# Second MoE, pairs 2 and 3 of 3: w_out by seven half-block products, four quads summed in PSUM, in an fp32r attention and two-MoE kernel

## The chip, the core and the metric

The kernel runs on one core of a Trainium2 chip. TensorE (PE in the profile; PEld is its weight load), VectorE (DVE), ScalarE (ACT), GpSimd (POOL) and SyncE (SP, which issues the DMAs here) work side by side and meet at semaphores. The metric is the device time of one execution in microseconds (us), lower is better.

## The reference

Linear attention with softmaxes over q and k, then two dense feed-forward layers ("MoE") on 2304 tokens, d_model 512, d_ff 2048. The second one is what the change touches:

```python
def _moe_ref(x, w_in, w_out):
    h = x @ w_in
    g = np.maximum(h, 0.0) + np.log1p(np.exp(-np.abs(h)))
    return (g @ w_out).astype(np.float32)

def _moe2_ref(x, w_in, w_out):
    h = x @ w_in
    alpha = 1.0
    g = np.where(h > 0.0, h, alpha * (np.exp(np.minimum(h, 0.0)) - 1.0))
    return (g @ w_out).astype(np.float32)
```

## The kernel before

Everything is float32 in and out; on PE a float32 number is a pair of fp32r values, high and low part, and a product is three matmuls (high x high, high x low, low x high). ACT makes the high part by a cast, DVE the low part by a subtraction.

Tokens go in six blocks of 384 (`BLK`, three rows `R` of 128); two blocks make a *pair* (p = 0, 1, 2 in names and code; pair 1, 2, 3 in words), d_ff is cut into eight *quads* `f` of 256 columns. The work unit is (MoE `m`, pair `p`, quad `f`), 48 in all; the second MoE is m = 1.

- **`up`** (`add_up`, L811): h = x @ w_in for two blocks and 256 columns by Strassen's scheme (Winograd's form): seven products instead of eight, six matmuls of 384 columns each, in the order 1, 2, 6, 5, 3, 7, 4 by due time. Products 1, 6, 5, 3 add into one PSUM bank `ub`, 2 into `ua`, 7 and 4 into `uc`; the ring `ha` has two banks. After 1, 6 and 5, ACT copies `ub` away to a tile `s`, and the next of these products adds to `ub` after that. DVE adds `s` to `ua` or `uc` and has `h`.
- **ELU** (`add_elu`): ACT relu(-h) and exp of that into `u`; DVE takes 1 off, then g = max(h, 0) + u.
- **Split** (`add_g`): `gh` by ACT, `gl` by DVE, for each half `j` of 128 d_ff columns.
- **Down** (`add_down`, L1016): plain: per quad 12 steps (two token blocks, two halves j, three rows r) of three matmuls with 512 columns, into six PSUM banks `acc0`, `acc1` that stay open over all eight quads of a pair. The first MoE's pairs 2 and 3 use `add_down_turned` (L978), where a matmul of 512 columns and one of 256 follow each other with the same weights, each with a load of its own.
- **Weights.** In m = 1, pair 1 builds the seven w_in forms and the high and low w_out of each quad and stores them to DRAM (`wfd`, 1.75 MB, and `wod`, 1 MB a quad); pairs 2 and 3 load them back (`wf`, `wo`, two buffers each).
- **End of a pair** (`add_store`): ACT and DVE copy the six banks to `y`, SP stores them.

Each operation is a step with an engine, a duration, what it reads and writes, the ring of buffers it takes, and a due time. `Plan.order` lists all steps: each engine takes next what can start first, and of those what is due first. The emitted order is that list, and every engine runs its part in order. `up` of one quad stands beside `down` of the quad before it.

Of the kernel before, what the change touches and what calls it, by code (L numbers as in the profile page):

```python
# [20 lines left out]
class Plan:  # L21
# [7 lines left out]
    def __init__(self, bufs):  # L29
        self.bufs = bufs  # L30
        self.steps, self.tile_ring, self.users = [], {}, {}
        self.writer, self.readers = {}, {}
        self.early, self.tab = 0.0, []

    def add(self, eng, dur, fn, r=(), w=(), new=(), due=None, after=0.0, behind=(), port=False, hold=(), tab=None):
        n = len(self.steps)
        deps = {i for i in behind if i is not None}
        for key, ring in new:
            self.tile_ring[key] = ring
        w = tuple(w) + tuple(key for key, _ in new)  # L40
# [12 lines left out]
        self.tab.append(tab)
        return n

    def order(self):
        n = len(self.steps)
        succ = [[] for _ in range(n)]
        for i, s in enumerate(self.steps):
            for d in s[3]:  # L60
                succ[d].append(i)
# [10 lines left out]
        free = {ring: [0.0] * c for ring, c in self.bufs.items()}  # L72
        ready = [0.0] * n
        clock = {PE: 0.0, ACT: 0.0, DVE: 0.0, POOL: 0.0, DMA: 0.0}
        open_ = {e: set() for e in clock}
        for i in range(n):
            if not left[i]:
                open_[self.steps[i][0]].add(i)
        lock, table = 0.0, "exp"
        seq = []  # L80
        while len(seq) < n:
            best = None
            for eng, cand in open_.items():
                starts = []
                for i in cand:
                    t = max(clock[eng], ready[i], lock if self.steps[i][-2] else 0.0)
                    if self.tab[i] not in (None, table):
                        t += T_TABLE
                    ok = True
                    need = {}  # L90
                    for _, ring in self.steps[i][4]:
                        need[ring] = need.get(ring, 0) + 1
                    for ring, c in need.items():
                        if len(free[ring]) < c:
                            ok = False
                            break
                        t = max(t, sorted(free[ring])[c - 1])
# [22 lines left out]
            for _, ring in new:  # L120
                free[ring].remove(min(free[ring]))
            for key in keys:
                uses[key] -= 1
                last[key] = max(last.get(key, 0.0), end)
                if not uses[key] and key in self.tile_ring:
                    free[self.tile_ring[key]].append(last[key] + SYNC)
# [30 lines left out]
def attention_moe_moe_kernel(  # L157
# [63 lines left out]
    const = pool("const")  # L221
    dp = pool("dp", bass.MemoryType.DRAM)

    plan = Plan({**{ring: b for ring, (b, _, _) in rings.items()}, **banks})
    T = {}

    def new(key, dt=None):
# [21 lines left out]
    }  # L249


    SLOT = 15.7
    UP, DN = 6 * 0.175, 3 * 0.231
    direct = lambda m, p, f: (m, p) == (0, 0) and f < 2
    quads = [(m, p, f) for m in range(2) for p in range(NPAIR) for f in range(NQ)]
    start, now = {}, 45.0
    for m, p, f in quads:
        start[m, p, f] = now
        now += SLOT + (3.0 if direct(m, p, f) else 0.0)
    end = now  # L260

    def after_quad(m, p, f):
# [481 lines left out]
    def add_w_out(m, f, rk):  # L744
# [9 lines left out]
        def _():  # L754
            nc.vector.tensor_tensor(
                T[wk][:, 2 * DM :], get(), T[wk][:, : 2 * DM].bitcast(F32), op=ALU.subtract
            )

        @step(DMA, 3.2, r=[hk, lk], w=[("wod", m, f)], hold=[wk], after=LAT)
# [30 lines left out]

    def add_up(m, p, f):
        t0 = start[m, p, f]
        wk = ("wf", m, "i", f, p)
# [4 lines left out]
        for i, at in ORDER:  # L798
            key, xk = where[i], ("xf", m, p, i)

            @step(
# [23 lines left out]

            elif i == 3:
                if m:
                    @step(ACT, t_act(BLK, True), r=[key], w=[("hp", m, p, f, 0, 1)], hold=[h0], behind=[made])
                    def _(key=key):
                        nc.scalar.copy(T[h0][:, BLK:], T[key][:, :BLK])  # L830
                else:
                    raw_h[p, f] = key

            else:
# [14 lines left out]
                made = _  # L849

    raw_h = {}

# [61 lines left out]
    def add_elu(p, f, j):  # L914

        hk, uk, gk = ((x, 1, p, f, j) for x in "hug")
        hs = [("hp", 1, p, f, j, half) for half in range(2)]

        @step(ACT, t_act(N2), r=hs, hold=[hk], make=[(uk, "u")], line="u")
        def _():  # L920
            nc.scalar.activation(new(uk), T[hk], AF.Relu, scale=-1.0)  # L921

        @step(ACT, t_act(N2), w=[uk], tab="exp")
        def _():
            nc.scalar.activation(T[uk], T[uk], AF.Exp, scale=-1.0)  # L925

        @step(DVE, t_dve(N2, True), w=[uk])
        def _():
            nc.vector.tensor_scalar(T[uk], T[uk], -1.0, None, op0=ALU.add)

        @step(DVE, t_dve(N2), r=[*hs, uk], hold=[hk], make=[(gk, "g")], line="g")
        def _():
            nc.vector.scalar_tensor_tensor(new(gk), T[hk], 0.0, T[uk], op0=ALU.max, op1=ALU.add)  # L933

    def add_g(m, p, f, j):
        gk, hk, lk = ((x, m, p, f, j) for x in ("g", "gh", "gl"))
# [47 lines left out]
    def add_down(m, p, f):  # L984
# [9 lines left out]
        for (i, j, r), at in zip(order, fill):  # L994
# [13 lines left out]
            def _(col=col, j=j, hk=hk, lk=lk, ak=ak, first=first, whole=whole, gk=gk, w32=w32):  # L1008
# [6 lines left out]
                for n, (g, a) in enumerate(((hk, 0), (hk, 1), (lk, 0))):  # L1015
# [95 lines left out]
    ahead = [(0, 1, 2), (0, 1, 4), (0, 1, 6), *((0, 2, f) for f in (0, 2, 3, 5, 6))]  # L1111

    for i, (m, p, f) in enumerate(quads):
        if f == 0:
            add_x(m, p)
        early(f"i{f}" if (m, p) == (0, 0) else "w")
# [10 lines left out]
        elif (m, p) == (0, 0):  # L1127
            add_w_out(m, f, add_words(m, "o", f))
        elif p == (1 if direct(m, 0, f) else 0):
            add_w_out(m, f, load_words(m, p, "o", f))  # L1130
        else:
            load_w_out(m, p, f)
        if (m, p, f) in ahead:
            early("ahead")
# [5 lines left out]
        else:  # L1140
            add_up(m, p, f)
            for j in range(2):
                (add_elu if m else add_softplus)(p, f, j)
                add_g(m, p, f, j)
        if i:
# [4 lines left out]
    add_down(*quads[-1])  # L1150
    add_store(*quads[-1][:2])

    with tc.manual_schedule():
        nc.scalar.preload_act_table_set("exp_and_others")
# [35 lines left out]
```

## Time and profile before

| | us |
|---|---|
| median of 3 runs | 842.66 (842.51 to 842.87) |
| span of the profiled execution | 841.3 |
| PE busy in it | 821.2 |
| DVE, ACT busy | 590.1, 534.2 |
| second MoE: pair 1, 2, 3 from about | 471.8, 597.2, 722.6 |

The span is from the first to the last instruction of the profiled execution; the timed runs hold what lies around it too. Busy times of the engines overlap.

### The profile page before, as it was taken

To read this page: it belongs to the slowest core of one execution; us is meant where nothing else is said; L and a number is where in the kernel's file an instruction comes from. 1 tells how busy PE (TensorE), PEld (TensorE's weight loads), DVE (VectorE), ACT (ScalarE), POOL (GpSimd) and SP (SyncE) were. 2 spreads that over 40 slices of the span, in tenths; PEclk is the share of its full clock that TensorE was granted. 3 is DMA by queue.
4 is the path that set the end of the run, shared out by engine and by line. 5 is a ranking of instruction groups with operands and counts; after the bars stand their busy time and mean duration, and the time that the engine had idled before them with its cause. 6 is when DMAs were issued, how large, how long until landed. Compare 5 with 4: busy or idle time off the path is not lost.

```text
span 841.3 us, 11929 instructions
## 1 busy us (share of the span) xinstructions
PE 821.2 (98%) x4678; PEld 721.3 (86%) x4678; DVE 590.1 (70%) x910; ACT 534.2 (63%) x786; POOL 6.1 (1%) x28
## 2 busy tenths in 40 slices
PE   5799999999999999999999999999999999999998
PEld 4466788889989999999999999899888899888896
DVE  7889999988888768776776786776544556533433
ACT  3877988886887757656655665665534456534443
POOL 2000000000000000000000000000000000000000
PEclk9999999999999999999999999999999999999999
DMA  9687775537885654687756689673765453763532
GB/s 283 165 280 248 216 261 194 199 100 238 263 310 181 236 205 161 221 303 267 250 178 230 261 300 338 257 295 143 250 234 216 179 232 139 255 232 138 187 139 76
DMA packets 63575, 186.37 MB, mean 222 GB/s; under 512 B 17952, under 2 KB 27168, under 8 KB 54560
## 3 DMA queue, kind: packets, MB, share of 16 engines
q1 hardware_dynamic: 63520, 185.61, 63.2%
q8 instruction: 37, 0.61, 0.3%
q14 instruction: 18, 0.15, 0.1%
HBM read 131.07 MB, written 54.53 MB: 221 GB/s over the span
## 4 chain that ended last, share of the span: by engine, by line
PE 83%; DVE 9%; ACT 5%; DMA 2%; issue 2%; ACTq 0%; DVEq 0%; SPq 0%
PE acc L1016 27%; PE ub L811 21%; PE acc L978 15%; PE uc L811 11%; PE ua L811 5%; PE px L507 1%; DMA raw_i<-in_moe_w_in_dram 1%; DMA raw_o<-in_moe_w_out_dram 1%; DVE mt L331 1%; PE pk L375 1%; DVE wf_i L731 1%; PE up L872 1%; ACT kvbd L401 1%; DVE ti_o L655 1%; PE pq L491 1%
## 5 line engine op out<-in xcount | busy, mean ns | idle before, releaser
L811 PE MATMUL ub<-xf,wf_i 128*128 128x384 f32 x1104 | 226.7, 340 | 0.4 <-ACT s L824 0.3
L1016 PE MATMUL acc<-wo_o,gh 128*128 128x512 f32 x720 | 226.0, 395 | 0.0
L811 PEld LDWEIGHTS ub<-xf,wf_i 128*128 128x128 f32 x1104 | 193.4, 188 | 16.5 <-ACT s L824 2.8
L845 DVE TENSOR_TENSOR h<-uc,s 128x384 f32<-128x384 f32 x92 | 51.1, 555 | 143.4 <-PE uc L811 135.0
L1016 PEld LDWEIGHTS acc<-wo_o,gh 128*128 128x128 f32 x720 | 132.5, 188 | 18.8
L1016 PE MATMUL acc<-wo_o,gl 128*128 128x512 f32 x360 | 142.5, 396 | 0.0
L824 ACT COPY s<-ub 128x384 f32<-128x384 f32 x138 | 65.9, 478 | 106.8 <-PE ub L811 106.5
L811 PE MATMUL uc<-xf,wf_i 128*128 128x384 f32 x552 | 112.2, 338 | 0.6 <-ACT g L893 0.6
L978 PE MATMUL acc<-gh,wo_o 128*128 128x512 f32 (+1 forms) x512 | 111.4, 339 | 0.0
L811 PEld LDWEIGHTS uc<-xf,wf_i 128*128 128x128 f32 x552 | 96.6, 188 | 8.2 <-ACT g L893 1.4
L940 ACT CAST gh<-g 128x768 fp32r<-128x768 f32 x92 | 77.1, 839 | 37.8 <-DVE g L933 37.1
L944 DVE TENSOR_TENSOR gl<-g,gh 128x768 fp32r<-128x768 f32 x92 | 87.8, 954 | 18.2 <-ACT gh L940 17.8
L978 PEld LDWEIGHTS acc<-gh,wo_o 128*128 128x128 f32 x512 | 83.2, 188 | 7.1
L1016 PEld LDWEIGHTS acc<-wo_o,gl 128*128 128x128 f32 x360 | 67.5, 187 | 14.4
L978 PE MATMUL acc<-gl,wo_o 128*128 128x512 f32 (+1 forms) x256 | 65.4, 336 | 0.0
L811 PE MATMUL ua<-xf,wf_i 128*128 128x384 f32 x276 | 55.8, 336 | 0.0
L811 PEld LDWEIGHTS ua<-xf,wf_i 128*128 128x128 f32 x276 | 48.0, 188 | 1.4 <-ACT xq L497 0.3
L933 DVE SCALAR_TENSOR_TENSOR g<-h,u 128x768 f32<-128x768 f32 x48 | 45.9, 957 | 1.4
L978 PEld LDWEIGHTS acc<-gl,wo_o 128*128 128x128 f32 x256 | 39.1, 188 | 5.3
L921 ACT ACTIVATE u<-h 128x768 f32<-128x768 f32 x48 | 40.7, 848 | 4.5 <-DVE h L845 2.7
L731 DVE TENSOR_TENSOR wf_i<-st_i,wf_i 128x1024 fp32r<-128x1024 f32 x30 | 36.6, 1221 | 8.1 <-ACT wf_i L727 7.9
L925 ACT ACTIVATE u<-u 128x768 f32<-128x768 f32 x48 | 40.7, 847 | 1.1
(98 smaller groups left out, 937.1 us busy)
## 6 DMA issues: line engine op xcount, KB each, us to landing
wo_o<-wod SPq DMA_DIRECT2D x30, 1024.0 KB, 6.8
wf_i<-wfd SPq DMA_DIRECT2D x16, 1792.0 KB, 7.3
raw_i<-in_moe_w_in_dram SPq DMA_DIRECT2D x16, 1024.0 KB, 6.5
raw_o<-in_moe_w_out_dram SPq DMA_DIRECT2D x16, 1024.0 KB, 7.4
wod<-wo_o SPq DMA_DIRECT2D x16, 1024.0 KB, 6.2
wfd<-wf_i SPq DMA_DIRECT2D x8, 1792.0 KB, 9.0
r_i<-w32i SPq DMA_DIRECT2D x24, 512.0 KB, 5.5
w32i<-ti_i SPq DMA_DIRECT2D x14, 512.0 KB, 5.5
```

The lines of the kernel that those rows point to most:

```text
L331: top = lambda o, x, y: nc.vector.tensor_tensor(o, x, y, op=ALU.max)
L731: nc.vector.tensor_tensor(view(1, lo, n, c), get(), view(0, lo, n, c).bitcast(F32), op=ALU.subtract)
L811: nc.tensor.matmul(ps[:, :BLK], T[wk][:, lo : lo + P], T[xk][:, (2 * c + kc) * BLK : (2 * c + kc + 1) * BLK], start=(i in first and kc == ...
L824: nc.scalar.copy(new(sk), T[key][:, :BLK])
L845: nc.vector.tensor_tensor(T[hk][:, half * BLK : (half + 1) * BLK], T[key][:, :BLK], T[sk], op=ALU.add)
L921: nc.scalar.activation(new(uk), T[hk], AF.Relu, scale=-1.0)
L925: nc.scalar.activation(T[uk], T[uk], AF.Exp, scale=-1.0)
L933: nc.vector.scalar_tensor_tensor(new(gk), T[hk], 0.0, T[uk], op0=ALU.max, op1=ALU.add)
L940: nc.scalar.copy(new(hk), T[gk])
L944: nc.vector.tensor_tensor(new(lk), T[gk], T[hk].bitcast(F32), op=ALU.subtract)
L978: nc.tensor.matmul(ps, T[wk][:, lo : lo + P], T[g][:, cols], start=(first and n == 0 and starts), stop=(f == NQ - 1 and j == 1 and n == 2) ...
L1016: nc.tensor.matmul(ps, T[g][:, col : col + P], T[wk][:, (2 * a + j) * DM : (2 * a + j + 1) * DM], start=(first and n == 0), stop=(f == NQ ...
```

## The change

For the second MoE's last two pairs (p = 1 and 2), `down` uses the same seven-product scheme. The g of a quad is a 2 x 2 matrix of blocks (two token blocks by two halves j), the w_out of it 2 x 2 (two halves j by two halves of 256 output columns). Four quads form a group, two groups a pair (`SIZES`).

- `add_elu`: g = max(exp(min(h, 0)) - 1, h) in one DVE pass; the separate -1 pass is gone in all of m = 1. In p = 1, 2 it is done in place in a buffer of the shared ring `G`.
- `add_parts`: for each quad, four sums of 384 columns on DVE, and for each of the seven products the operand's high part (ACT) and low part (DVE) into one of six buffers `F`. `add_g` is not called for these quads.
- `add_products`: products in the order 1, 7, 6, 2, 5, 4, 3; each loads one 1 MB weight tile `ws` for all four quads, and per quad runs nine matmuls of 256 columns (a *product step*: six for rows 0 and 1 in a bank of `acc0`, three for row 2 in a bank of `acc1`), summing four quads in PSUM. Then the bank is read out and set or added into rows `Y` in SBUF: ACT for products 1, 6, 7, 3 of a pair's first group, DVE for the rest. Rows go out by DMA when a pair is complete.
- `add_sums`: in pair 1 (p = 0) the four block sums of w_out, their splits, and six stores a quad into the DRAM tile `wos`, in place of the store to `wod`.
- `add_claims`: after p = 0, idle buffers of other rings (`u`, `g`, `gh`, `gl`, `ti`, `st`, `k`, `v`, `q`, `xq`, `yl`, `raw`, `y`) are given to the rings `G`, `F`, `S`, `Y`; in the order they are named `claim_` with the old ring's name.
- The products of a group stand beside `up` of the next group; those of the last group stand alone. `SLOT` goes from 15.7 to 15.666, which moves due times everywhere a little.

```diff
-        @step(DVE, t_dve(N2, True), w=[uk])
-        def _():
-            nc.vector.tensor_scalar(T[uk], T[uk], -1.0, None, op0=ALU.add)
-
-        @step(DVE, t_dve(N2), r=[*hs, uk], hold=[hk], make=[(gk, "g")], line="g")
...
+            nc.vector.scalar_tensor_tensor(
+                T[gk] if uk == gk else new(gk), T[uk], -1.0, T[hk], op0=ALU.add, op1=ALU.max
+            )
...
+    def add_parts(m, p, i, f):
...
+        if i == 7:
+            sum_(lambda: slot(sk), lambda: block(1), lambda: block(3), ALU.add, [b21, b22], [], gk, [(sk, "S")])
+            sum_(lambda: block(1), lambda: block(0), lambda: block(1), ALU.subtract, [b11], [b21], gk[:1])
+        if i == 6:
+            sum_(lambda: block(0), s, lambda: block(0), ALU.subtract, [sk], [b11], gk[:1])
+        if i == 3:
+            sum_(lambda: block(2), lambda: block(2), lambda: block(0), ALU.subtract, [b11], [b12], gk)
...
+        @step(ACT, t_act(BLK), r=[key], make=[(fk, "F")], w=[fh], hold=hold, line="F")
+        def _():
+            nc.scalar.copy(halves(fk)[0], get())
+
+        @step(DVE, t_dve(BLK), r=[key, fh], w=[fl], hold=[fk, *hold])
+        def _():
+            nc.vector.tensor_tensor(T[fk][1], get(), T[fk][0].bitcast(F32), op=ALU.subtract)
...
+    def add_products(m, p, fs):
...
+        for n, i in enumerate(PRODUCTS):
+            ck = ("ws", m, p, gi, i)
+            spare = n % 2 and final
+            @step(
+                DMA, t_dma(P * K * DM * 4), r=[("wosd", m, f) for f in fs], after=LAT, make=[(ck, "wf" if spare else "wo")],
+                behind=[last_up[quads[-2]]] if spare else begun[-2:-1] or [plan.maker["wo"]],
+            )
...
+            for part, rs in enumerate(((0, 1), (2,))):
+                for q, f in enumerate(fs):
...
+                        for x, r in enumerate(rs):
+                            for c, (a, b) in enumerate(((0, 0), (0, 1), (1, 0))):
+                                nc.tensor.matmul(
+                                    ps[:, x * 256 : x * 256 + 256], T[fk][a][:, r * P : (r + 1) * P],
+                                    T[ck][:, q * 512 + b * 256 : q * 512 + b * 256 + 256],
...
+                    if opens:
+                        nc.scalar.copy(o, a)
+                    else:
+                        nc.vector.tensor_tensor(o, a, o, op=ALU.add)
```

Where the order changes, three places. Names end with a running number; `ub_1_1_2` is the bank `ub` of (m 1, p 1, f 2), `xf_1_1_6` the form of x for product 6, `acc` the open banks, `Pb`, `Pc` the product banks (m, p, first quad of the group, part), `ws_1_2_4_1` the weights of product 1 of the group that starts with quad 4.

PE, `up` of quad (1, 1, 2) before: down steps of the quads before stand between its products.

```order
L811 MATMUL ub_1_1_2_5996<-xf_1_1_1_5625,wf_1_i_2_1_5856 128x384 x6
L811 MATMUL ua_1_1_2_6007<-xf_1_1_2_5633,wf_1_i_2_1_5856 128x384 x6
L1016 MATMUL acc_1_1_1_2_6017<-wo_1_o_0_1_5786,gh_1_1_0_0_5854 128x512 x2
L1016 MATMUL acc_1_1_1_2_6017<-wo_1_o_0_1_5786,gl_1_1_0_0_5862 128x512
L1016 MATMUL acc_1_1_1_2_6017<-wo_1_o_0_1_5786,gh_1_1_0_1_5894 128x512 x2
L1016 MATMUL acc_1_1_1_2_6017<-wo_1_o_0_1_5786,gl_1_1_0_1_5910 128x512
L1016 MATMUL acc_1_1_0_0_5896<-wo_1_o_1_1_5908,gh_1_1_1_0_5990 128x512 x2
L1016 MATMUL acc_1_1_0_0_5896<-wo_1_o_1_1_5908,gl_1_1_1_0_6003 128x512
L811 MATMUL ub_1_1_2_5996<-xf_1_1_6_5648,wf_1_i_2_1_5856 128x384 x6
L1016 MATMUL acc_1_1_0_1_5912<-wo_1_o_1_1_5908,gh_1_1_1_0_5990 128x512 x2
L1016 MATMUL acc_1_1_0_1_5912<-wo_1_o_1_1_5908,gl_1_1_1_0_6003 128x512
```

The same quad now, and the first products of the next one.

```order
L1185 MATMUL Pb_1_1_0_0_6061<-ws_1_1_0_1_5908,claim_q_0_3026 128x256 x6
L833 MATMUL ub_1_1_2_6072<-xf_1_1_1_5737,wf_1_i_2_1_5970 128x384 x6
L833 MATMUL ua_1_1_2_6080<-xf_1_1_2_5745,wf_1_i_2_1_5970 128x384 x6
L1185 MATMUL Pb_1_1_0_1_6091<-ws_1_1_0_1_5908,claim_q_0_3026 128x256 x3
L833 MATMUL ub_1_1_2_6072<-xf_1_1_6_5761,wf_1_i_2_1_5970 128x384 x6
L833 MATMUL ub_1_1_2_6072<-xf_1_1_5_5789,wf_1_i_2_1_5970 128x384 x6
L833 MATMUL uc_1_1_2_6117<-xf_1_1_7_5826,wf_1_i_2_1_5970 128x384 x6
L833 MATMUL ub_1_1_2_6072<-xf_1_1_3_5819,wf_1_i_2_1_5970 128x384 x6
L833 MATMUL uc_1_1_2_6117<-xf_1_1_4_5855,wf_1_i_2_1_5970 128x384 x6
L833 MATMUL ub_1_1_3_6145<-xf_1_1_1_5737,wf_1_i_3_1_6070 128x384 x6
L833 MATMUL ua_1_1_3_6158<-xf_1_1_2_5745,wf_1_i_3_1_6070 128x384 x6
L833 MATMUL ub_1_1_3_6145<-xf_1_1_6_5761,wf_1_i_3_1_6070 128x384 x6
```

Only one product step, of the first quad, lies between the `up` products; 5 stands right behind 6 on `ub`.

PE, where the last `up` ends. Now, from `up` 3 of quad (1, 2, 7) on (before, its `up` 4 is followed by 7 steps of the quad before and then 12 steps of its own quad):

```order
L833 MATMUL ub_1_2_7_7957<-xf_1_2_3_6805,wf_1_i_7_2_7801 128x384 x6
L1185 MATMUL Pb_1_2_0_0_7495<-ws_1_2_0_3_7940,claim_k_0_5810 128x256 x6
L1185 MATMUL Pb_1_2_0_1_7505<-ws_1_2_0_3_7940,claim_k_0_5810 128x256 x3
L833 MATMUL uc_1_2_7_8048<-xf_1_2_4_6866,wf_1_i_7_2_7801 128x384 x6
L1185 MATMUL Pb_1_2_0_0_7495<-ws_1_2_0_3_7940,claim_v_0_5818 128x256 x6
L1185 MATMUL Pb_1_2_0_1_7505<-ws_1_2_0_3_7940,claim_v_0_5818 128x256 x3
L1185 MATMUL Pb_1_2_4_0_8107<-ws_1_2_4_1_8032,claim_q_0_3026 128x256 x6
L1185 MATMUL Pb_1_2_4_1_8115<-ws_1_2_4_1_8032,claim_q_0_3026 128x256 x3
```

Behind these rows stand product 1 of quads 5, 6, 7 and then products 7, 6, 2, 5, 4, 3 of the four quads, 28 product steps with the first shown here, and no `up`.

DVE at the same place, now, from the max of the last quad's first half on (the rows of L1116 are block sums, of L1139 low parts, of L1210 read-outs):

```order
L960 SCALAR_TENSOR_TENSOR claim_gh_1_5959<-claim_gh_1_5959,h_1_2_7_0_7996 128x768
L1139 TENSOR_TENSOR claim_st_0_5666<-claim_gh_1_5959,claim_st_0_5666 128x384
L960 SCALAR_TENSOR_TENSOR claim_ti_0_5670<-claim_ti_0_5670,h_1_2_7_1_8063 128x768
L1139 TENSOR_TENSOR claim_k_0_5810<-claim_gl_1_5960,claim_k_0_5810 128x384
L1139 TENSOR_TENSOR claim_v_0_5818<-claim_u_0_5885,claim_v_0_5818 128x384
L1116 TENSOR_TENSOR claim_y_1_6255<-claim_gh_1_5959,claim_ti_0_5670 128x384
L1139 TENSOR_TENSOR claim_q_0_3026<-claim_ti_1_5729,claim_q_0_3026 128x384
L1116 TENSOR_TENSOR claim_gh_1_5959<-claim_gh_1_5959 128x384
L1210 TENSOR_TENSOR claim_raw_1_5748<-Pb_1_2_4_0_8107,claim_raw_1_5748 128x2x256
L1210 TENSOR_TENSOR claim_raw_1_5748<-Pb_1_2_4_1_8115,claim_raw_1_5748 128x256
L1139 TENSOR_TENSOR claim_xq_1_3365<-claim_gh_1_5959,claim_xq_0_3355 128x384
```

From the first of these rows to the end DVE has 48 instructions: 2 of the max, 7 block sums, 25 low parts, 14 read-outs. Before, only the last quad's -1 pass, max and low part and three read-outs stood there.

## Rows read from the trace of the kernel before

**Rows 1.** The page's busy time, share of the span and instructions by engine.
```profile
PE 821.2 (98%) x4678; PEld 721.3 (86%) x4678; DVE 590.1 (70%) x910; ACT 534.2 (63%) x786; POOL 6.1 (1%) x28
```
**Rows 2.** Busy time (us) by engine in stretches; then PE clock, DMA share, GB/s.
```profile
60.00:120.00 60.00, 59.14 (x309) 43.72 (x308) 59.56 (x91) 51.12 (x69) 0.13 (x1) 1.00 0.77 248
...
440.00:471.00 31.00, 31.00 (x180) 29.02 (x179) 22.35 (x34) 20.92 (x32) 0.00 (x0) 1.00 0.64 234
...
471.80:597.15 125.35, 125.35 (x626) 112.75 (x625) 89.22 (x131) 77.48 (x113) 0.00 (x0) 1.00 0.72 269
597.15:722.60 125.45, 125.43 (x624) 112.52 (x624) 62.35 (x86) 61.59 (x90) 0.00 (x0) 1.00 0.56 209
```
**Rows 3.** Waits from 597 us on: us in total, times, longest.
```profile
ACT s L824 <- PE ub L811: 64.2, 40, 2.0
...
PEld uc L811 <- DVE h L845: 0.9, 2, 0.5
```
**Rows 4.** Groups by line, shapes apart: busy us, mean ns of one, idle before.
```profile
L811 PEld LDWEIGHTS ub<-xf,wf_i 128*128 128x128 f32 x1104 | 193.4, 188 | 16.5 <-ACT s L824 2.8 <-issue 1.8
...
L944 DVE TENSOR_TENSOR gl<-g,gh 128x768 fp32r<-128x768 f32 x92 | 87.8, 954 | 18.2 <-ACT gh L940 17.8
L940 ACT CAST gh<-g 128x768 fp32r<-128x768 f32 x92 | 77.1, 839 | 37.8 <-DVE g L933 37.1
...
L824 ACT COPY s<-ub 128x384 f32<-128x384 f32 x138 | 65.9, 478 | 106.8 <-PE ub L811 106.5
...
L845 DVE TENSOR_TENSOR h<-uc,s 128x384 f32<-128x384 f32 x92 | 51.1, 555 | 143.4 <-PE uc L811 135.0 <-ACT u L921 4.5 <-ACT g L893 3.7
...
L933 DVE SCALAR_TENSOR_TENSOR g<-h,u 128x768 f32<-128x768 f32 x48 | 45.9, 957 | 1.4
L921 ACT ACTIVATE u<-h 128x768 f32<-128x768 f32 x48 | 40.7, 848 | 4.5 <-DVE h L845 2.7
...
L929 DVE TENSOR_SCALAR u<-u 128x768 f32<-128x768 f32 x48 | 26.6, 555 | 13.5 <-ACT u L925 13.5
...
L711 DVE TENSOR_TENSOR st_i<-r_i 128x256 f32<-128x256 f32 x48 | 20.1, 419 | 0.9 <-DMA r_i<-w32i 0.9
...
L893 ACT ACTIVATE g<-h 128x384 f32<-128x384 f32 x22 | 11.6, 525 | 4.6 <-DVE h L845 4.4
...
L1067 DVE COPY y<-acc 128x512 f32<-128x512 f32 x11 | 7.5, 685 | 3.1 <-PE acc L1016 3.0
```
**Rows 5.** The chain that ended last, in order of time: start us, us, what.
```profile
448.20 2.08 PE acc L978 x12
...
496.54 2.76 PE acc L1016 x12
...
512.23 2.76 PE acc L1016 x12
```
**Rows 6.** PE's instructions in order of time: start us, us, line, shapes.
```profile
404.50 0.60 PE L551 MATMUL py<-ident,yl 128*128 128x128 f32 x4
404.85 0.95 PE L978 MATMUL acc<-gh,wo_o 128*128 128x512 f32 x4
405.63 0.51 PE L978 MATMUL acc<-gl,wo_o 128*128 128x512 f32 x2
405.99 0.60 PE L551 MATMUL py<-ident,yl 128*128 128x128 f32 x4
```
**Rows 7.** The end of the program in order of time.
```profile
837.53 0.42 DVE L1067 COPY y<-acc 128x256 f32<-128x256 f32 x1 [0.67 <-PE acc L1016]
837.98 0.37 ACT L1067 COPY y<-acc 128x256 f32<-128x256 f32 x1 [0.55 <-DVE y L1067]
```
**Rows 8.** Landing of the second MoE's w_out loads; DMA issues, KB each, us.
```profile
L781 SPq DMA_DIRECT2D wo_o<-wod x15: 319/319/327, 593.5 to 813.7; - x15
...
DMA to landing us min/median/max: 4.8/6.9/8.6
...
wf_i<-wfd SPq DMA_DIRECT2D x16, 1792.0 KB, 7.3
```

More of the change, by code (lines that the diff above doesn't have):

```diff
@@ L33, in __init__ @@
         self.early, self.tab = 0.0, []
+        self.maker, self.gives, self.place = {}, {}, {}
     def add(self, eng, dur, fn, r=(), w=(), new=(), due=None, after=0.0, behind=(), port=False, hold=(), tab=None):
         n = len(self.steps)
+        for _, ring in new:
+            self.maker[ring] = n
         deps = {i for i in behind if i is not None}
@@ L71, in order @@
         last = {}
-        free = {ring: [0.0] * c for ring, c in self.bufs.items()}
+        free = {ring: [(0.0, i) for i in range(c)] for ring, c in self.bufs.items()}
         ready = [0.0] * n
@@ L119, in order @@
                 lock = t + dur
-            for _, ring in new:
-                free[ring].remove(min(free[ring]))
+            for key, ring in new:
+                slot = min(free[ring])
+                free[ring].remove(slot)
+                self.place[key] = slot[1]
+            for ring, slot in self.gives.get(i, ()):
+                free[ring].append((end, slot))
             for key in keys:
@@ L249, in attention_moe_moe_kernel @@
     }
-    SLOT = 15.7
-    UP, DN = 6 * 0.175, 3 * 0.231
+    UP, DN, DS = 6 * 0.175, 3 * 0.231, 3 * R * 0.118
+    SLOT = 7 * UP + 4 * R * DN
+    SIZES = {(1, 1): (4, 4), (1, 2): (4, 4)}
     direct = lambda m, p, f: (m, p) == (0, 0) and f < 2
+    seven = lambda m, p: (m, p) in SIZES
+    groups = [(m, p, tuple(range(sum(n[:i]), sum(n[: i + 1])))) for (m, p), n in SIZES.items() for i in range(len(n))]
+    group = {(m, p, f): i for i, (m, p, fs) in enumerate(groups) for f in fs}
     quads = [(m, p, f) for m in range(2) for p in range(NPAIR) for f in range(NQ)]
-    start, now = {}, 45.0
-    for m, p, f in quads:
+    start, beside, now = {}, {}, 45.0
+    for i, (m, p, f) in enumerate(quads):
         start[m, p, f] = now
-        now += SLOT + (3.0 if direct(m, p, f) else 0.0)
+        before, own = (len(groups[group[x]][2]) if x in group else 0 for x in (
+            groups[group[m, p, f] - 1][:2] + (groups[group[m, p, f] - 1][2][0],) if group.get((m, p, f)) else None, (m, p, f)
+        ))
+        beside[m, p, f] = 4 * R * DN if i and quads[i - 1] not in group else 7 * DS * before / own if own else 0.0
+        now += 7 * UP + (beside[m, p, f] or (4 * R * DN if not i else 0.0)) + (3.0 if direct(m, p, f) else 0.0)
     end = now
@@ L757, in _ @@
             )
+        if seven(m, 1):
+            return
         @step(DMA, 3.2, r=[hk, lk], w=[("wod", m, f)], hold=[wk], after=LAT)
@@ L792, in add_up @@
         t0 = start[m, p, f]
+        other = beside[m, p, f]
         wk = ("wf", m, "i", f, p)
@@ L797, in add_up @@
         h0 = ("h", m, p, f, 0)
-        for i, at in ORDER:
+        order = ORDER
+        if quads.index((m, p, f)) and other < 4 * R * DN:
+            order = [(i, n * (UP + other / 7)) for n, i in enumerate((1, 2, 6, 5, 7, 3, 4))]
+        for i, at in order:
             key, xk = where[i], ("xf", m, p, i)
@@ L827, in add_up @@
                 if m:
-                    @step(ACT, t_act(BLK, True), r=[key], w=[("hp", m, p, f, 0, 1)], hold=[h0], behind=[made])
+                    @step(ACT, t_act(BLK, True), r=[key], w=[("hp", m, p, f, 0, 1)], hold=[h0], behind=[opened])
                     def _(key=key):
@@ L917, in add_elu @@
         hs = [("hp", 1, p, f, j, half) for half in range(2)]
-        @step(ACT, t_act(N2), r=hs, hold=[hk], make=[(uk, "u")], line="u")
+        if seven(1, p):
+            uk = gk
+        @step(ACT, t_act(N2), r=hs, hold=[hk], make=[(uk, "G" if uk == gk else "u")], line="u")
         def _():
-            nc.scalar.activation(new(uk), T[hk], AF.Relu, scale=-1.0)
+            nc.scalar.activation(slot(uk) if uk == gk else new(uk), T[hk], AF.Relu, scale=-1.0)
         @step(ACT, t_act(N2), w=[uk], tab="exp")
@@ L1020, in _, with claim @@
                     )
+    def claim(ring, *give):
+        key = ("claim", ring, len(claims[ring]))
+        claims[ring].append(key)
+        @step(POOL, 0.0, make=[(key, ring)], behind=[plan.maker.get(ring)])
+        def _():
+            rounded = give[0][0][0] == "F"
+            t = new(key, F32R if rounded else F32)
+            for name, n, lo, hi in give:
+                views[name, n] = t[:, lo:hi]
+        plan.users[key].append(-1)
+        plan.gives[_] = [(name, n) for name, n, _, _ in give if name != "F1"]
+        return _
@@ L1113, in attention_moe_moe_kernel @@
     for i, (m, p, f) in enumerate(quads):
+        if i and seven(m, p) and not seven(*quads[i - 1][:2]):
+            m_, p_, f_ = quads[i - 1]
+            add_down(m_, p_, f_)
+            add_store(m_, p_)
+            add_claims()
         if f == 0:
@@ L1129, in attention_moe_moe_kernel @@
         elif p == (1 if direct(m, 0, f) else 0):
-            add_w_out(m, f, load_words(m, p, "o", f))
-        else:
+            rk = load_words(m, p, "o", f)
+            add_w_out(m, f, rk)
+            if seven(m, 1):
+                add_sums(m, f, rk)
+        elif not seven(m, p):
             load_w_out(m, p, f)
@@ L1143, in attention_moe_moe_kernel @@
                 (add_elu if m else add_softplus)(p, f, j)
-                add_g(m, p, f, j)
-        if i:
+                if not seven(m, p):
+                    add_g(m, p, f, j)
+        if i and not seven(m, p):
             m_, p_, f_ = quads[i - 1]
@@ L1149, in attention_moe_moe_kernel @@
                 add_store(m_, p_)
-    add_down(*quads[-1])
-    add_store(*quads[-1][:2])
+        fs = groups[group[m, p, f]][2] if (m, p, f) in group else ()
+        if f in fs[-1:]:
+            for n in PRODUCTS:
+                for f_ in fs:
+                    add_parts(m, p, n, f_)
+            add_products(m, p, fs)
     with tc.manual_schedule():
```

164 lines of the change are left out of this document (159 added, 5 removed).

## The prediction

> **What bounds the kernel now.** I read the page's busy shares first: PE is busy for 821.2 of 841.3 us [rows 1]. A busy PE need not be at its best, so I went on to the stages. The busy time by stretch [rows 2] gives the second MoE's pair 1 (471.80 to 597.15 us) and pair 2 (597.15 to 722.60): the clock is granted in full (1.00), PE is busy for 125.35 of 125.35 and 125.43 of 125.45 us, DVE for 89.22 and 62.35, ACT for 77.48 and 61.59. Then the waits from 597 us to the end [rows 3]: ACT waits 64.2 us for PE in one group alone, while the longest entry in which PE's side waits for anybody is 0.9 us in total. So in this stretch only PE's own work counts; a column of matmul taken away is time taken away, as long as the other engines keep up. One quad takes 512.23 - 496.54 = 15.69 us, by the distance of two equal pieces of the chain [rows 5].
>
> **What the matmuls cost.** The chain has twelve 512-column matmuls in 2.76 us, 0.230 each, and in the turned part twelve that alternate 512 and 256 columns in 2.08 us: six pairs of 0.347, which leaves 0.1167 for the 256-column one [rows 5]. The change replaces, for each of 16 quads, 12 steps of 3 matmuls with 512 columns (36 x 0.230 = 8.28 us) by 7 products of 9 matmuls with 256 columns (63 x 0.1167 = 7.35 us). That is 0.93 a quad, **-14.9 us** over 16. The seven `up` products stay as they are, at (15.69 - 8.28) / 7 = 1.06 us a step.
>
> No row shows 256-column matmuls back to back, each with a load of its own. From below, columns alone at the 512 rate give 0.115 (then -16.6 us in all). From above stands the weight load: a record of one lasts 188 ns [rows 4], more than 117. Two things speak against reading that as the load's hold on the engine. In the turned pairs two loads fit into 0.347 us. And four 128-column transposes with six of these matmuls take 405.99 - 404.50 = 1.49 us [rows 6], of which the six take 1.04, so a transpose with its 128-column load takes 0.1125; its columns alone would take half of 0.1167, so that 0.1125 is about what a load costs in a row of loads. I take 0.1167 and keep the other as a rival. The Trainium skill (TensorE: Matmul & The Clock Gate, section LDWEIGHTS) gives a load's columns divided by 1.2 in ns, 107 for 128 columns, whereas the record here is 188 and the transposes' spacing about 112; by 107 the sum stays as it is, by 188 it turns over (below).
>
> **What the other engines get.** In pairs 2 and 3 each quad loses two casts on ACT (0.839), two subtractions (0.954) and two -1 passes (0.555) on DVE, and gains seven casts of 384 (ACT, 0.525), and seven subtractions and four block sums of 384 (DVE, 0.555) [rows 4]. A pair also gets 14 products to read out, in two pieces of 512 and 256 columns: 10 on DVE (0.685 and at least 0.419), 4 on ACT. For pair 2 DVE goes from 62.35 to 62.35 - 24.1 + 48.8 + 11.0 - 2.1 (three old read-outs) = 96 us, in about 118 us of PE work: 81%. Pair 1 prepares the seven weight blocks: four sums (0.419) and two splits of 512 (0.685) a quad, 24.4 us, less 8.9 for the -1 passes: DVE 104.7 of 125.35, 84%. Here the order moves almost nothing on PE. What such shares cost is bounded by the stretch from 60 to 120 us, where DVE was busy for 59.56 of 60.00 us and PE still for 59.14 [rows 2]: 0.86 us in 60, so 0 to 3.5 us over pairs 1 to 3. I take **+0.7**. The shorter ELU takes 48 passes of 0.555 from DVE; the PE work that covers all of ELU hides them, so it counts for nothing except in these shares.
>
> **Where PE loses its filler.** The first four quads of pair 2 have no product beside them until their own operands exist. In the order, quad (1,1,2) runs its seven `up` steps in a row, and product 5 directly follows product 6 into the same bank, so PE waits for ACT's copy of that bank (0.478 us), perhaps behind a 0.848 us pass on ACT [rows 4]. In (1,1,3) a product step stands between them. I count one such stop: **+0.8**, bounds 0.5 and 2.
>
> **The last four quads** have no `up` beside them: 28 product steps of 9 x 0.1167 = 1.05 us, 29.4 us, fed by DVE. From the last quad's max on, DVE's order has 48 instructions: 2 of 0.957, 32 of 0.555, 7 of 0.685, 7 of 0.419, 27.4 us. That is just under PE's 29.4, with ACT's casts beside it. Two chains could be late. The last operand of product 1 needs copy, relu, exponential, max, cast, subtraction after `up` 3: 0.478 + 0.848 + 0.848 + 0.957 + 0.525 + 0.555 = 4.2 us; six steps of 1.05 us cover it, 6.3. The last operand of product 7 needs after `up` 4 an add, two passes for each half (3.4 at most), max, two sums, cast and subtraction: 0.555 + 3.4 + 0.957 + 1.11 + 0.525 + 0.555 = 7.1 against eight steps, 8.4. Covered with 1.3 to spare: **+0.5**, bounds 0 and 3. What is queued behind a late operand is the whole rest of PE's list, so lateness there is paid in full.
>
> **The end.** Before, the last accumulator is read in two halves, from 837.53 to 838.35 [rows 7]. Now DVE reads a 512-column piece and then the 256 columns: 0.685 + 0.419 instead of 0.82, and three stores leave together. **+0.3**, bounds 0 and 1.5.
>
> **Transfers.** A product's weights are 1 MB, in two buffers, so a load has to land while one other product runs: 4 x 1.05 us of it and about 4 `up` steps, 8.4 us. The same size took 4.8/6.9/8.6 us to land (shortest, middle, longest), the 1.75 MB `up` weights 7.3 in the middle [rows 8]. On SP's queue a load that waits for its buffer holds up the `up` weights behind it. Sizes 1.75 and 1 MB with 7.3 and 4.8 us mean 3.3 us a MB and 1.5 fixed: a product's load right behind an `up` load would need 10.6, 2.2 too late. I expect the middle case: **+0.4**, bounds 0 and 4. In pair 1 six stores of 0.25 to 0.5 MB, 1.75 MB in all, replace one of 1 MB a quad; nobody waits for them before pair 2.
>
> **Sum.** -14.9 + 0.7 + 0.8 + 0.5 + 0.3 + 0.4 = -12.2: the span goes from 841.3 to 829.1. The runs' median is 842.66, 1.4 above that span, so I predict **830.5 us**. All costs at their lower bounds and the dearer 256-column price give 828.3; with 0.115 us for 256 columns 826.6.
>
> **Rivals.**
> First, *the weight loads become the bound*. For each quad there are 42 + 63 = 105 loads, before 78. PE's loads are busy for 112.52 of 125.45 us in pair 2, 0.90 [rows 2]; at 0.188 each, 63 products' matmuls would take 11.84 instead of 8.28 a quad, +57 us, about 900. The point from which the change loses is 8.28/63 = 0.131 us for a load. In the turned stretch 440 to 471 the loads are busy for 29.02 us over 179, 0.162 each, while matmuls come closer together, so the records overlap; with the transposes this speaks against it: 5%. The Trainium skill (Perfetto Trace Analysis, section Identifying the Most-Contended Engine) takes the busy share of weight loads as a measure of how near TensorE is to its limit; by that rule 0.90 leaves little room and 105 loads of 188 ns, 19.7 us, do not fit into a quad. The turned stretch, where 0.162 is less than a record, shows that rule too strict here.
> Second, *the operand chain is late* in the last or the first group, or DVE and ACT, at 81 and 84%, stop PE now and then: several of the upper bounds above come together, 4 to 10 us are lost, 834 to 841. For it: DVE's 27.4 against 29.4. Against it: the 60 to 120 us row. 17%.
> Third, *the loads are late in every quad*, 2.2 us on 14 quads, 31 us: that eats the gain at 0.9 us a quad and would give about 846 to 860; half of it no change. Against it: the longest landing so far is 8.6. 4% no change, 2% slower.
> My own case, 827 to 834 us: 72%.
>
> **How the numbers follow.** Faster by over 0.2% (1.7 us, about what a measurement of this kernel can tell from nothing) are the main and the second case and a little beyond: 0.90. Within 0.2%: 0.04. Slower: the loads of either kind, 0.06. The range reaches from 826.6, the cheap 256 columns, to 836, which leaves out the worse half of the second case and the rest: 82% inside.
>
> **What would show it.** In the profile after: 256-column matmuls at 0.117 us a piece in the chain; quads in the middle of pairs 2 and 3 at about 14.8 us; a wait of PE for `s` in (1,1,2); hardly a wait of PE for the casts in the last 30 us. Nine product matmuls in clearly more than 1.05 us without a wait would show the weight loads. Waits of PE for the cast or subtraction of operands would show the second rival, waits for the product's weights the third; any of them of more than 6 us in total proves me wrong.

## The result, and the profile after

The changed kernel takes 832.61 us (median of 4 runs, 832.39 to 833.62) beside 842.76 (842.51 to 844.02): a ratio of 0.9881, 95% interval 0.9867 to 0.9895. The prediction was 830.5, range 826.6 to 836.0. The profiled execution, the longest of the four, spans 831.9 us, 9.4 less than before; the sum of the prediction had said 12.2.

The page's busy time by engine:

```profile
PE 809.3 (97%) x5110; PEld 732.4 (88%) x5110; DVE 657.5 (79%) x1088; ACT 564.7 (68%) x889; POOL 6.1 (1%) x28
```

PE lost 11.9 us against [rows 1], DVE gained 67. Busy time by stretch, columns as in [rows 2]; the second MoE's pair 1, the first group of pair 2, the middle, and the last four quads with the end:

```profile
474.04:597.00 122.96, 122.96 (x614) 110.76 (x614) 96.39 (x155) 81.95 (x124) 0.00 (x0) 1.00 0.84 305
597.00:630.00 33.00, 32.03 (x193) 30.86 (x192) 20.80 (x36) 21.22 (x38) 0.00 (x0) 1.00 0.89 310
630.00:795.95 165.95, 165.95 (x1179) 165.89 (x1178) 122.20 (x217) 103.01 (x187) 0.00 (x0) 1.00 0.70 253
795.95:831.90 35.95, 31.17 (x261) 30.96 (x260) 24.71 (x49) 14.41 (x30) 0.00 (x0) 1.00 0.51 191
```

In these four stretches PE waits only between 597 and 630 us; for 166 us behind that it never does, though DVE is busy for 74% and the weight loads' records fill the stretch. The waits from 597 us on, columns as in [rows 3], name PE's side four times:

```profile
PEld ub L833 <- ACT s L846: 1.3, 2, 0.9
...
PE ub L833 <- ACT s L846: 0.8, 2, 0.6
...
PEld ub L833 <- issue: 0.5, 1, 0.5
...
PE ub L833 <- DMA wf_i<-wfd: 0.2, 1, 0.2
```

The chain gives the prices, as [rows 5] did (start us, us, what): quad (1,1,7) with the product steps between its `up` steps, then a product of the last group, 36 matmuls of 256 columns.

```profile
663.85 1.04 PE ub L833 x6
664.89 1.07 PE Pc L1185 x9
665.96 1.04 PE ua L833 x6
...
678.66 0.35 PE ub L833 x2
...
809.92 4.29 PE Pa L1185 x36
```

A product step takes 1.07 us (1.05 predicted), an `up` step 1.04 (1.06), a quad 14.81; four quads from 722.87 to 782.07 us give 14.80 against 15.69: 0.89 a quad.

Where the rest went is seen by setting the starts of the same `up` steps side by side. PE in order of time, before, at quads (0,0,7) and (0,2,2):

```profile
164.44 0.68 PE L811 MATMUL ub<-xf,wf_i 128*128 128x384 f32 x3
...
351.65 0.68 PE L811 MATMUL ub<-xf,wf_i 128*128 128x384 f32 x3
```

and in the changed kernel, with the two PE waits that the trace names in between, and below them the waits in quads (1,1,2) and (1,1,4):

```profile
164.51 0.68 PE L833 MATMUL ub<-xf,wf_i 128*128 128x384 f32 x3
...
208.49 0.33 PE L354 MATMUL pt<-ident,mx 128*128 128x128 f32 x1 [0.42 <-DVE h L867]
...
230.82 0.96 PE L833 MATMUL uc<-xf,wf_i 128*128 128x384 f32 x4 [0.58 <-ACT g L916]
...
353.87 0.68 PE L833 MATMUL ub<-xf,wf_i 128*128 128x384 f32 x3
...
606.08 1.22 PE L833 MATMUL ub<-xf,wf_i 128*128 128x384 f32 x6
607.87 1.31 PE L833 MATMUL ub<-xf,wf_i 128*128 128x384 f32 x6 [0.57 <-ACT s L846]
...
625.54 1.15 PE L833 MATMUL ub<-xf,wf_i 128*128 128x384 f32 x5 [0.22 <-ACT s L846]
```

The first MoE, whose mathematics nobody touched, is 2.2 us longer between these two places, with the same matmuls in between. The two waits are 1.0 of it; the rest is spread over smaller stops and was not traced to single places. In (1,1,2) an `up` step of 1.04 us is followed by the next after 1.79.

The end in order of time, as [rows 7]:

```profile
826.72 0.40 PE L1185 MATMUL Pb<-ws,claim_st 128*128 128x256 f32 x2
826.80 1.02 DVE L1210 TENSOR_TENSOR claim_raw<-Pb,claim_raw 128x512 f32<-128x512 f32 x2 [3.27 <-PE Pb L1185]
827.52 1.30 SPq L1223 DMA_DIRECT2D out_dram<-claim_raw  x3
```

The last of the two matmuls starts at 826.84, and from its end (start plus 0.12) at 826.96 it takes 4.95 us to the end of the span; before, the last matmul ended at 837.33 and 4.0 us were left.

The account against the prediction's terms, in us of span:

| term | predicted | measured |
|---|---|---|
| matmuls of 16 quads | -14.9 | -14.2 (16 x 0.89) |
| DVE's and ACT's share | +0.7 | 0.0 |
| pair 2's first four quads | +0.8 | +1.3 |
| last group's operands | +0.5 | 0.0 |
| transfers | +0.4 | +0.4 |
| end | +0.3 | +0.9 |
| order of the first MoE | not there | +2.2 |
| sum | -12.2 | -9.4 |

### The profile page after: what moved, and what is told of

The parts are those of the page before. It is cut to its first block, busy times and chain, and to the rows that moved or that the text cites. A ratio compares the mean times of both kernels' runs of the same rounds, so it can differ in the third digit from the quotient of the medians.

```text
span 831.9 us, 13270 instructions
## 1 busy us (share of the span) xinstructions
PE 809.3 (97%) x5110; PEld 732.4 (88%) x5110; DVE 657.5 (79%) x1088; ACT 564.7 (68%) x889; POOL 6.1 (1%) x28
## 4 chain that ended last, share of the span: by engine, by line
PE 82%; DVE 8%; ACT 5%; DMA 2%; issue 2%; DVEq 0%; ACTq 0%; SPq 0%
PE ub L833 21%; PE acc L1007 15%; PE acc L1045 13%; PE uc L833 11%; PE Pb L1185 8%; PE ua L833 5%; PE Pc L1185 4%; PE Pa L1185 2%; PE px L522 1%; DMA wf_i<-wfd 1%; DVE mt L346 1%; PE acc L1040 1%; PE pk L390 1%; DMA raw_i<-in_moe_w_in_dram 1%; PE pq L506 1%
## 5 line engine op out<-in xcount | busy, mean ns | idle before, releaser
L833 PEld LDWEIGHTS ub<-xf,wf_i 128*128 128x128 f32 x1104 | 189.3, 188 | 13.4 <-ACT s L846 4.3
L1045 PE MATMUL acc<-wo_o,gh 128*128 128x512 f32 x336 | 106.7, 398 | 0.0
L1045 PEld LDWEIGHTS acc<-wo_o,gh 128*128 128x128 f32 x336 | 61.4, 188 | 9.0 <-ACT yt L1295 0.2
L1045 PE MATMUL acc<-wo_o,gl 128*128 128x512 f32 x168 | 66.5, 396 | 0.0
L973 DVE TENSOR_TENSOR gl<-g,gh 128x768 fp32r<-128x768 f32 x60 | 57.2, 953 | 8.4 <-ACT gh L969 8.3
L969 ACT CAST gh<-g 128x768 fp32r<-128x768 f32 x60 | 50.2, 836 | 7.1 <-DVE g L960 6.3
L916 ACT ACTIVATE g<-h 128x384 f32<-128x384 f32 (+1 forms) x44 | 30.2, 686 | 16.3 <-DVE h L867 16.1
L1045 PEld LDWEIGHTS acc<-wo_o,gl 128*128 128x128 f32 x168 | 31.5, 187 | 6.8
L742 ACT CAST wf_i<-r_i 128x512 fp32r<-128x512 f32 (+1 forms) x48 | 23.2, 511 | 16.5 <-PE uc L833 16.4
L742 ACT CAST wf_i<-st_i 128x1024 fp32r<-128x1024 f32 x30 | 31.4, 1048 | 1.1 <-DVE st_i L726 1.0
```

Source lines behind the costliest of these rows:

```text
L742: nc.scalar.copy(view(0, lo, n, c), get())
L833: nc.tensor.matmul(ps[:, :BLK], T[wk][:, lo : lo + P], T[xk][:, (2 * c + kc) * BLK : (2 * c + kc + 1) * BLK], start=(i in first and kc == ...
L916: nc.scalar.activation(o, i, AF.Softplus)
L969: nc.scalar.copy(new(hk), T[gk])
L973: nc.vector.tensor_tensor(new(lk), T[gk], T[hk].bitcast(F32), op=ALU.subtract)
L1045: nc.tensor.matmul(ps, T[g][:, col : col + P], T[wk][:, (2 * a + j) * DM : (2 * a + j + 1) * DM], start=(first and n == 0), stop=(f == NQ ...
```

## Experiments

Two questions were open: what made the first MoE longer, and whether 256-column matmuls are dearer than read or weight loads are near. Theory for the first: the new distance of quads in the plan, 15.666 us for 15.7, reorders its steps. Rivals: scatter, or the new stores.

**The distance alone**, on the kernel before:

```diff
-    SLOT = 15.7
-    UP, DN = 6 * 0.175, 3 * 0.231
+    UP, DN = 6 * 0.175, 3 * 0.231
+    SLOT = 7 * UP + 4 * 3 * DN
```

> The kernel before with the planned distance of quads alone changed, 15.666 us in place of 15.7. Theory (the order did it): PE's order in the first MoE becomes that of the changed kernel, the second MoE begins 2.2 us later, 845.0 us (844.4 to 845.6). Rival (the due times do nothing by themselves): 842.8.

846.46 us beside 843.55, ratio 1.0031 (1.0022 to 1.0040): slower by 2.6 us at the base of 842.7. The same two `up` steps:

```profile
165.28 0.87 PE L811 MATMUL ub<-xf,wf_i 128*128 128x384 f32 x4
...
354.58 0.68 PE L811 MATMUL ub<-xf,wf_i 128*128 128x384 f32 x3
```

It is 189.30 us between them, 187.21 before and 189.36 in the changed kernel, and the same two waits of 0.4 and 0.6 us stand there. So 34 ns in the plan's distance cost 2.1 us in a part that the change doesn't name.

**The old distance in the changed kernel:**

```diff
-        now += 7 * UP + (beside[m, p, f] or ...) + ...
+        now += (7 * UP + beside[m, p, f] if own else 15.7) + ...
```

> The changed kernel with the planned starts of all quads ahead of the second MoE's pair 2 set 15.7 us apart again, in place of 15.666; nothing else is touched. In the program PE's order is then that of before up to the last quad of the first MoE. Theory (the order did it): the 2.2 us by which the second MoE began later in the changed kernel (474.04 against 471.80 us) come from the reordered steps of the first MoE, so its first steps start at 471.8 again and the time falls by 2.2, from 832.6 to 830.4 us (829.9 to 831.0). Rival (the later start is scatter of the profiled execution, or the price of the new stores): no change, 832.6.

Half right. Quad (0,2,2) starts at 351.76, as before; but the time is 834.24 us beside 843.55, a ratio of 0.9888 (0.9871 to 0.9905): no gain over the changed kernel. PE, and below it ACT, in the second MoE's second quad:

```profile
469.98 1.21 PE L833 MATMUL ub<-xf,wf_i 128*128 128x384 f32 x6
472.20 1.32 PE L833 MATMUL ub<-xf,wf_i 128*128 128x384 f32 x6 [1.01 <-ACT s L846]
474.55 1.34 PE L833 MATMUL ub<-xf,wf_i 128*128 128x384 f32 x6 [1.04 <-ACT s L846]
...
461.20 0.62 ACT L1260 CAST wk<-T 128x512 fp32r<-128x512 f32 x1
...
462.46 0.61 ACT L1260 CAST wv<-T 128x512 fp32r<-128x512 f32 x1
...
469.64 1.28 ACT L950 ACT_TABLE_LOAD   x1
```

The same table load before, and then in the changed kernel:

```profile
462.10 1.28 ACT L925 ACT_TABLE_LOAD   x1
...
466.56 1.28 ACT L950 ACT_TABLE_LOAD   x1
```

Busy time by engine around the stop, columns as in [rows 2]:

```profile
468.00:478.00 10.00, 7.95 (x42) 6.92 (x41) 7.91 (x11) 9.22 (x14) 0.00 (x0) 1.00 1.01 388
```

Products 1, 2, 6, 5, 3 stand in a row with no down step between, since the first down operands are late: the ACT table for the exponential is loaded at 469.64, against 462.10 before and 466.56 in the changed kernel. The plan (`T_TABLE`) charges a table change 1.3 us, so in the plan ACT takes whatever can start without one; the casts of the new weight blocks (L1260) are two more such steps.

**The weight sums later**, on top of it (the expectation calls it the second quad; the gate is the last `up` step of the second MoE's first quad, (1,0,0)):

```diff
-            @step(DVE, t_dve(256), r=[rk], ...
+            @step(DVE, t_dve(256), behind=[last_up[m, 0, 0]], r=[rk], ...
```

with `add_sums` called behind `add_up` of its quad.

> The changed kernel with the starts 15.7 us apart as in the first experiment, and the sums of the seven weight blocks not allowed before the last up step of the second MoE's second quad. In the program PE's order is that of before through the first MoE and into that quad, and a down step stands again between its products 6, 5 and 3. Theory (the sums on DVE and ACT made the first down operands late, and that used up what the order gave back): no PE wait of over 0.2 us between 470 and 476 us, and the second MoE's quads up to the end of its pair 1 begin within 0.3 us of before; 2.2 to 2.6 us less than the first experiment and than the changed kernel, a span of 829.4 us and a time near 830.3. Rival (something else, the six stores for instance, holds PE there): the 2.6 us stay, span 831.9.

830.92 us beside 842.49, ratio 0.9858 (0.9844 to 0.9873); span 829.8. ACT's table load and first exponential in order of time, and then the busy time by engine in the stretch where PE stood still:

```profile
462.43 1.28 ACT L950 ACT_TABLE_LOAD   x1
463.72 0.85 ACT L950 ACTIVATE u<-u 128x768 f32<-128x768 f32 x1
```

```profile
468.00:478.00 10.00, 10.00 (x54) 9.32 (x53) 8.10 (x15) 6.23 (x12) 0.00 (x0) 1.00 0.73 225
```

With the table load back near its old place, PE is busy for 10.00 of 10.00 us (7.95 in the run before this one), and the quads begin 0.3 us from before up to pair 2. So the plan's order cost 2.2 us, and the sums, put late, cost nothing on PE: in the trace all of the 2.2 us came back. In time it is 1.65 us less than the changed kernel run beside it (830.25 to 831.81 against 832.34 to 832.71), short of the 2.2 to 2.6 expected. The sums on DVE, their casts on ACT and the stores behind them moved together, so which of them pushed the table load back is read from ACT's order and was not tested one by one.

**Price of 256 columns**, on the kernel before:

```diff
-                    nc.tensor.matmul(ps, ..., T[wk][:, (2 * a + j) * DM : (2 * a + j + 1) * DM], ...)
+                    for lo, hi in zip(parts, parts[1:]):   # (0, 256, 512) for pairs 2 and 3
+                        nc.tensor.matmul(ps[:, lo:hi], ..., T[wk][:, (2 * a + j) * DM + lo : (2 * a + j) * DM + hi], ...)
```

> The kernel before, with each 512-column matmul of the down product in the second MoE's pairs 2 and 3 written as two of 256 columns with the same weights, 72 in place of 36 a quad, in the same order; DVE, ACT and the transfers are untouched. This is the price of 256-column matmuls in a row by itself. Theory (0.119 us is the price of such a matmul, whatever feeds it): 72 x 0.1192 - 36 x 0.230 = 0.30 a quad, 4.8 over 16, 847.6 us. By the prediction's 0.1167: 0.12 a quad, 844.7 us. If weight loads were the bound from 0.131 us on: 1.15 a quad, 861 us or more.

Ratio 1.0029 (1.0018 to 1.0039), 2.4 us more. The chain, and the busy time from 640 to 800 us:

```profile
653.03 1.04 PE uc L811 x6
654.07 2.87 PE acc L1018 x24
...
668.91 1.04 PE uc L811 x6
```

```profile
640.00:800.00 160.00, 159.99 (x1150) 159.78 (x1150) 75.60 (x105) 75.70 (x111) 0.00 (x0) 1.00 0.52 192
```

2.87/24 = 0.1196: the price belongs to the matmul, not to the operands' supply, as DVE and ACT have their old work here. The total misses the expected 4.8, since `up` steps fell from 1.06 to 1.04 us: a quad went from 15.69 to 15.88, 0.19 x 16 = 3.0. By the time alone the prediction's 0.1167 (2.0 us more) would fit as well; the chain tells the two apart.

**Where loads bind:** the same with four matmuls of 128 columns.

```diff
-                parts = (0, DM // 2, DM) if m and p else (0, DM)
+                parts = range(0, DM + 1, DM // 4) if m and p else (0, DM)
```

> The kernel before, with each 512-column matmul of the down product in the second MoE's pairs 2 and 3 written as four of 128 columns with the same weights, 144 a quad. This looks for the point where weight loads become the bound. Theory (a load holds TensorE for less than 0.119 us, about the 0.1125 that a transpose takes with its load): 0.1125 a matmul, 16.2 us in place of 8.3 a quad, 7.9 us x 16 = 126 us more, about 969 us. If a load held it for 0.06 or less: 0.06 a matmul, some 6 us more, 849 us.

966.42 us (one run) beside 842.49, 123.9 more, 7.74 a quad: (8.30 + 7.74)/144 = 0.111 us a matmul. Its stretch from 640 to 760 us:

```profile
640.00:760.00 120.00, 120.00 (x948) 120.00 (x947) 40.97 (x56) 39.70 (x58) 0.00 (x0) 1.00 0.38 135
```

By their columns alone these matmuls would take a quarter of 0.230, 0.058 us. So a matmul with a load of 128 columns of its own has a floor of 0.111 us here, and 256 columns at 0.119 are 7% above it. That the load sets the floor, and not the issue of the pair, is the likely reading; no run separates the two. By the Trainium skill (TensorE: Matmul & The Clock Gate, section LDWEIGHTS) a load takes its columns divided by 1.2 in ns, an estimate of 107 ns; the run agrees within 4%.

**The shorter ELU alone**, on the kernel before: one DVE pass (`uk - 1`, then max with h) for two.

> The kernel before with the shorter ELU alone, in all three pairs of the second MoE: the -1 pass goes and the last pass does it with the max. Theory (hidden by PE): DVE's busy time falls by 48 x 0.555 = 26.6 us and the time stays within 0.1%, 842.0 to 843.5. Rival (operands were late now and then): up to 1 us less in the second MoE, 841.7.

842.89 beside 843.55, ratio 0.9994 (0.9984 to 1.0003); DVE's busy time falls from 590.1 to 563.8 us. No gain that can be told from nothing, as the prediction costed it. The interval alone would leave room for the rival's 1 us, but in the trace the same `up` step of quads (1,0,3) and (1,2,7) lies 314.34 us apart before and 314.31 with the shorter ELU.

**The first group and the end**, on the kernel with the later sums:

```diff
+                    if final and n == 6:
+                        at = due(4 * n) + DS * ((4 * 2 + q) / 3 if part else q * 2 / 3)
...
+                        behind=[up_step[m, p, 2, 6]] if n == q == group[m, p, gi] == 0 else [],
```

> As the run with the later sums, and two more moves of steps: both pieces of product 1 for the first quad of pair 2's first group wait until after product 6 of quad (1,1,2), so that they stand between products 6 and 5; and the last product of all runs its 512-column piece over all four quads first and its 256-column piece behind it, so that only the small read-out and one store are left at the end. Theory (these are the two other places where the changed kernel lost time): the wait of 0.73 us in quad (1,1,2) falls to under 0.2, and from the last matmul's start to the end of the span it takes about 4.0 us in place of 5.0; together 1.3 to 1.7 us less than the run with the later sums, a span near 828.0. Rival (the end is the landing of stores whatever stands ahead): the end stays at 5.0 and only 0.5 us are won.

830.76 us, ratio 0.9856 (0.9841 to 0.9871), span 828.3. The wait in (1,1,2) is gone, but the end stayed long, as the rival had it: 5.11 us from the last matmul's start. The last store was issued 0.8 us sooner and landed as late. To tell scatter from order, the same again, and each part alone:

> The kernel with the filler and the reordered last product once more. In its first profile the last store was issued 0.77 us after the last matmul's start, against 1.59 in the changed kernel, but took 3.40 us to land, against 2.47 there and 2.03 in the kernel before. If that landing is scatter of one execution, it is 2.0 to 2.1 us here and the end from the last matmul's start takes 3.8 us; if it belongs to the new order of stores, it is 3.4 again and the end takes 5.1.

> The kernel with the later sums and the reordered last product, without the moved filler. Theory: the wait of 0.73 us between products 6 and 5 of quad (1,1,2) is back; the end is as in the run beside it, since it has the same steps. The filler alone is then worth 0.5 to 0.7 us of the start of pair 3 and the reordered end 1.2 where the last store lands in 2.0 us; the time lies at 830.0 to 830.9, 0.5 above the run beside it.

> The kernel with the later sums and the moved filler, with the last product in the order of the changed kernel. The three runs with the reordered last product all had a last store that took 3.3 to 3.4 us to land. If that belongs to that order, here the last store lands in 2.4 to 2.5 us and from the last matmul's start to the end it takes 5.0 to 5.3 us as in the changed kernel, the same as with the reordered end. The filler gives 0.5 us against the run with the later sums: from the first up step of quad (0,1,0) to the end the trace is 0.5 us shorter than there, the time 830.3 to 830.9.

Ratios 0.9855 (0.9839 to 0.9871), 0.9864 (0.9848 to 0.9881) and 0.9855 (0.9837 to 0.9872); medians 830.75, 831.69 and 830.46 us. With the reordered end the last store took 3.39, 3.39 and 3.31 us to land, so it is no scatter; without it 2.47 (changed) and 2.48 (filler alone), where two others are issued just ahead. The last store in the repeat, and then in the run with the filler alone (KB, us to landing):

```profile
out_dram<-claim_raw SPq DMA_DIRECT2D x1, 256.0 KB, 3.4
```

```profile
out_dram<-claim_raw SPq DMA_DIRECT2D x1, 256.0 KB, 2.5
```

The end took 5.11, 5.11 and 5.03 us with the reorder; without it 5.01 to 5.32 in five profiles (5.08 in the changed kernel, 5.31 with the filler alone). So of the 1.2 us expected nothing can be told from scatter. Why the store lands later is open. The filler gave 0.6 us of span, counted from the start of quad (0,1,0) to leave the beginning out (645.22 to 644.62); in time no run with either edit can be told from the run with the later sums, and the tail alone came 0.8 above what was expected, 0.4 of it a late product load in the profiled execution.

**The changed kernel again:**

> The changed kernel once more, beside the others on one chip: 0.988 of before, 832 to 834 us, so that the runs of this call can be compared with it.

832.57, ratio 0.9878 (0.9861 to 0.9894), span 830.6. Its first MoE lost 2.2 us between the same two quads, 163.44 to 352.85. The versions with the later sums are the best: 1.4% under the kernel before, against 1.2% for the change as it is; the intervals of these ratios overlap a little, the times of the runs made beside each other do not.

## Why the prediction was right, and where it was off

**What bounds it:** right. PE's own work sets the end, no helper stops it in the middle, and 0.89 us a quad came out where 0.93 was forecast.

**The matmuls:** right in kind, mis-sized by 0.7 of 14.9. 0.1167 was a difference of two group prices; in a row of their own such matmuls take 0.119 (1.07/9) to 0.1196 us (2.87/24), which alone would be some 2 us dearer. The cheaper `up` steps beside them gave most of that back.

**DVE's and ACT's share (+0.7), the last operands (+0.5):** nothing was lost. The stretch from 60 to 120 us, where DVE is busy for 99%, was a poor measure for an engine at 74 to 78%, and the upper bound of 3.5 does not follow from it: 0.86 in 60 us would be 5.2 over the some 361 us of three pairs.

**First group (+0.8):** the wait in (1,1,2) came where it was placed, at 0.85 us with its follow-on. A second one of 0.49 at 625 us in (1,1,4), also for ACT's copy, was not foreseen: only the smaller piece of a product step (three matmuls, 0.35 us) stands between products 6 and 5 there.

**Transfers (+0.4):** one `up` load was late by 0.4 in this execution. Of the seven later profiles of the changed kind, two (the repeat and the tail alone) have a stop of 0.2 to 0.3 at the start of quad (1,1,4), where the `up` load had just landed; the others have none. The product loads, the third rival, took 4.7, 5.4 and 9.1 us to land (shortest, middle, longest). They were late once in all of these, by 0.4 us, when one took 11.6 us from issue to landing (the tail alone): not a bound, but with little to spare. The 10.6 us of the prediction rested on a slope between a shortest landing (4.8) and a middle one (7.3), which are not alike; with 6.9, the middle one of the smaller load, it would be 0.5 us a MB and 6.4 fixed.

**The end (+0.3):** 0.9, and for another reason. The read-outs took 1.02 us together, near the 1.10 of the sum, but the first begins ahead of the last matmul's end, so they are done 0.87 us behind it, sooner than before (1.03). The three stores were named and given no price: the last is issued at 828.43, 0.60 us behind the read-out (0.02 before), and takes 2.47 us to land, against 2.02.

**The step that failed** is one that is not in the sum: the first MoE. The due times move with `SLOT`, and they were costed at nothing; the list of three places where the order changes leaves the first MoE out. The runs with the distance alone and with the old distance show 2.1 to 2.2 us for it, the largest error by far. The other errors come to 0.6 together. That 832.6 us lies in the range is owed to room that was left for late operands, not to this term.

**The rivals:** weight loads as the bound fell: the break-even of 0.131 us stands above the 0.119 measured and the floor of 0.111. By the Trainium skill's rule (Perfetto Trace Analysis, section Identifying the Most-Contended Engine) the busy share of loads tells the headroom. With 256 columns it is 1.00 (165.89 of 165.95 us) and a matmul takes 0.119 us, 0.004 over half of a 512-column one, so the measurement decides against it here. In the second MoE, operands of `down` stopped PE for more than 0.2 us in one run only, the one with the old distance: the exponential came late behind ACT's table load, and DVE waited for it (1.3 us).

## What to carry to other kernels

Price a matmul from a row of the same shape in the same company, and expect the neighbours' price to move too. Where a planner sets the order, compare the orders of all engines in all stages, also where the change has no business, and cost what moved; a constant that shifts due times by 0.2% cost more here than any other error. Where an engine has a costly switch (a table), a plan that charges the switch can let cheap steps that need none push it back until somebody waits.

## What was not expected of the hardware

- Weight loads' records were busy for 1.00 of the time at 256 columns (0.119 us a matmul) and at 128 (0.111). A record lasts 188 to 192 ns in both and overlaps the next ones, so this share does not tell that only the second is held by something other than its columns.
- The last store of 256 KB took 2.0 us to land when those before it were spread out (but 2.63 in the run with the distance alone, in the same order), 2.5 as the third of three together, 3.3 to 3.4 as a third issued 0.8 us behind the second of two others. The cause is open.
- The same order begins up to 1 us apart from execution to execution: quad (0,0,7) at 163.44 and 164.51 us in two profiles of the changed kernel. The distance from there to quad (0,2,2) is 189.41 and 189.36 us.
